# Splitting the product A22 T4 by quarters as well, in blocks two and three

## Chip, core and metric

One core of a Trainium2 chip. The metric is the device time of one launch in microseconds, median of the runs. The engines are called as in the profile: PE (TensorE matmuls), PEld (its weight loads), DVE (VectorE), ACT (ScalarE), POOL (GpSimd), SP (the queue that issues nearly all DMAs).

## What is computed

Local attention over 3072 tokens, then a dense layer pair, then a soft mixture of eight experts whose gate is balanced by eight Sinkhorn rounds. The change lies in the last stage alone:

```python
for e in range(8):
    h = np.maximum(x @ w1[e], 0.0)      # 3072x512 @ 512x1024
    ye = h @ w2[e]                      # 3072x1024 @ 1024x512
    out += P[:, e:e + 1] * ye
```

## The kernel before

The expert stage walks over 24 units `n`: three blocks of 1024 tokens (`sb`), in each eight experts (`e`). Both matrix products of a unit are done by Winograd's form of Strassen's scheme: seven products of half-size matrices instead of eight. Every float32 product is three matmuls in fp32r (`passes`, L225 to L227: high by high, high by low, low by high), each with its own weight load.

For the first product the seven are listed in `FIRST` (weight part, token part, accumulator): 0 is A12 B21 on accumulator b, 1 is A11 B11 on a, 2 is S1 T1 on c, 3 is S2 T2 on a, 4 is S3 T3 on a, 5 is S4 B22 on c, 6 is A22 T4 on a. The accumulators are PSUM tiles that are read out after each product and then added to, so that a product on `a` has to wait until the one before it on `a` has been read.

A plain product takes four steps (`k` = 0 to 3, one per 128 rows of the result), each with six matmuls of 512 columns. Product 0 is split once more: `deep_product` does it as seven sub-products of quarter matrices, again by `FIRST`, in four steps of up to two sub-products (`SUBS`): 1 and 0, 2 and 3, 5 and 4, then 6. A sub-product is six matmuls of 256 columns. The read-outs are in `deep_out` (L876 on ACT, L878 on DVE), those of plain products in `first_out` (L887, L889 on ACT, L891 on DVE); `positive` (L897) takes the Relu, and `gated` (L904) multiplies by the gate on POOL.

A list `order` sets one step of the first product of unit n beside one step of the second product of unit n-1; a unit is 28 steps. In a plain step PE runs six matmuls of the first product and then six of the second. In a deep step it runs a sub-product, half of the second product's step (three matmuls), the other sub-product, and the other half. In the order of the steps of `USES` the deep steps 0, 1 and 2 of product 0 stand first, then two plain steps of product 1, then deep step 3:

```python
    SUBS = ((1, 0), (2, 3), (5, 4), (6,))
    USES = [(DEEP, 0), (DEEP, 1), (DEEP, 2), (0, 1), (DEEP, 3)]
    USES += [(k, p) for k in (0, 2) for p in range(1, 7) if k or p > 1]
```

The weight parts w1 of the next uses are loaded ahead (`w1_load`), rounded to fp32r by ACT (`w1_hi`, L781), and their rest is taken by DVE in block one (`w1_lo`, L786) and stored, and read back in the blocks behind it (`w1_lo_load`). The sums of weight parts (S1 to S4) are made once, on POOL, by the jobs of `factory` during the stages ahead, each a load of 512 KB, four POOL operations (L636) and a store of 512 KB. `gate_load` fetches a unit's gate (tile `pb`). For a new block the token parts are split half by half (`x_half`), those of B21 by quarters (`x_quarters`).

Of the kernel before, what the change touches and what calls it, by code (L numbers as in the profile page):

```python
# [9 lines left out]
F32 = mybir.dt.float32  # L10
# [22 lines left out]
HB = 512  # L33
NEG = -2.0 ** 100
LAG = 2
NG = 14
# [28 lines left out]
def attn_moe_moe(ctx: ExitStack, tc: tile.TileContext, qk, vw, wi, wo, wa, wb, wg, out):  # L65
# [538 lines left out]
    DEEP = "deep"  # L604
    QUART = {"B11": 0, "B21": 1, "B22": 2, "T1": 3, "T3": 4, "T4": 5, "T2": 6}
    SUBS = ((1, 0), (2, 3), (5, 4), (6,))
    USES = [(DEEP, 0), (DEEP, 1), (DEEP, 2), (0, 1), (DEEP, 3)]
    USES += [(k, p) for k in (0, 2) for p in range(1, 7) if k or p > 1]
    NW = 16 * NM
# [14 lines left out]
    def factory():  # L624
# [27 lines left out]
    def quarter_tile():  # L652
        xo["B21"] = xo_p.tile([128, 2, 7, 256], F32R, tag="xoB21", name="xo", bufs=1)

    def quarter_parts(names, raw):
        t, at = xo["B21"], QUART[names[0]]
        hi, lo = (t[:, v, at:at + len(names)].rearrange("p a t -> p (a t)") for v in range(2))
        nc.scalar.activation(out=hi, in_=raw, func=AF.Copy)
        nc.vector.tensor_tensor(out=lo, in0=raw, in1=hi.bitcast(F32), op=ALU.subtract)
# [4 lines left out]
    def x_quarters(r0, r1, eng=nc.vector):  # L664

        l, h = slice(0, 256), slice(256, 512)
        quarter_tile()
        quarter_parts(("B11",), r0[:, l])
        quarter_parts(("B21", "B22"), r1)
# [4 lines left out]
        quarter_parts(("T1", "T3"), r0)  # L674
# [4 lines left out]
        quarter_parts(("T4", "T2"), r1)  # L679
        yield  # L680

    def x_ops(sb, p, tag):
# [24 lines left out]
        yield from x_quarters(xq["B21"][:, 0], xq["B21"][:, 1])  # L707
# [24 lines left out]
    def x_half_load(sb, r):  # L732

        if r < 14:
# [18 lines left out]
    def w1_use(g):  # L753
        return g // 16 % NE, *USES[g % 16]

    def w1_load(g):
        if g < NW:
            e, k, p = w1_use(g)
            s = w1s[g] = w1s_p.tile([128, 2, 256], F32, tag="w1s", name="w1s", bufs=4)
            wk = wa[4 * e:4 * e + 4].rearrange("k p (a f) -> p k a f", a=4)  # L760
            if k == DEEP and p in (1, 2):
                for j in range(2):
                    nc.sync.dma_start(out=s[:, j].rearrange("p (k f) -> p k f", k=2),
                                      in_=quarter(ws3[e], W3S[S1 + 2 * p - 2 + j]))
            elif k == DEEP:
# [590 lines left out]
```

## Time and profile before

| what | value |
|---|---|
| median of 3 runs | 2508.99 us (2508.58 to 2509.62) |
| the profiled execution's own time | 2509.49 us |
| its span, first to last instruction | 2507.7 us |
| busy PE, PEld | 2493.5 us, 2164.3 us |
| busy DVE, ACT, POOL | 1790.2 us, 1416.9 us, 978.1 us |
| mean granted TensorE clock | 1.000 |
| DMA moved | 569.84 MB, mean 227 GB/s |
| expert stage | from about 659 us to the end |

Block one of the expert stage ends near 1246 us, block two near 1856 us. A matmul's end is modelled, so two that follow each other overlap in the rows; what a matmul costs is the distance from its start to the start of the next.

### The profile page before, as it was taken

How to read it: one execution, taken by the hardware profiler on the slowest of the kernel's cores; microseconds unless marked ns; L12 is line 12 of the kernel's file. 1: busy time of each engine (PE TensorE's matmuls, PEld its weight loads, DVE VectorE, ACT ScalarE, POOL GpSimd, SP SyncE). 2: the span in 40 equal slices, each digit the busy share in tenths (PEclk: the TensorE clock that was granted, in tenths of full speed). 3: DMA queues.
4: the chain of work that ended last, by engine and by line, in shares of the span. 5: the costliest groups of instructions: out<-in, count | busy, mean ns of one | idle time of the engine just before them, and what ended most of it. 6: DMA issues, size and time to landing. Idle time of an engine off the chain costs nothing.

```text
span 2507.7 us, 36585 instructions
## 1 busy us (share of the span) xinstructions
PE 2493.5 (99%) x13237; PEld 2164.3 (86%) x13237; DVE 1790.2 (71%) x2252; ACT 1416.9 (57%) x2611; POOL 978.1 (39%) x729
## 2 busy tenths in 40 slices
PE   9999999999999999999999999999999999999999
PEld 8999999999878888888888888888888888888887
DVE  8777656576699999999975656566675566666567
ACT  8666652222365655556666555655566656555554
POOL 0155656454025544433443424333333334233331
PEclk9999999999999999999999999999999999999999
DMA  8689988676466676667777777666686666666654
GB/s 210 188 264 307 288 268 275 228 268 216 135 222 212 237 230 240 227 222 231 248 232 246 236 230 239 226 214 215 218 272 214 221 219 213 202 216 210 213 189 148
DMA packets 344305, 569.84 MB, mean 227 GB/s; under 512 B 28531, under 2 KB 198716, under 8 KB 344124
## 3 DMA queue, kind: packets, MB, share of 16 engines
q1 hardware_dynamic: 343840, 567.28, 69.6%
q8 instruction: 103, 1.69, 0.3%
q14 instruction: 78, 0.64, 0.1%
q10 hardware_dynamic: 284, 0.24, 0.0%
HBM read 434.13 MB, written 133.27 MB: 226 GB/s over the span
## 4 chain that ended last, share of the span: by engine, by line
PE 94%; DVE 4%; ACT 1%; DMA 1%; issue 1%; ACTq 0%; SPq 0%; DVEq 0%
PE ga L225 8%; PE ga L227 7%; PE ga L226 7%; PE oa L226 7%; PE oa L225 7%; PE oa L227 7%; PE gc L225 4%; PE pa L225 4%; PE gc L226 4%; PE gc L227 4%; PE oc L226 4%; PE ph L225 4%; PE pa L227 3%; PE pa L226 3%; PE oc L227 3%; PE oc L225 3%
## 5 line engine op out<-in xcount | busy, mean ns | idle before, releaser
L904 POOL TENSOR_TENSOR g<-g,pb 128x512 f32<-128x512 f32 x368 | 637.1, 1745 | 1148.2 <-ACT g L897 1060.2
L940 ACT ACTIVATE oh<-g 128x1024 fp32r<-128x1024 f32 x336 | 355.0, 1056 | 508.6 <-issue 191.7
L945 DVE TENSOR_TENSOR ol<-g,oh 128x1024 fp32r<-128x1024 f32 x336 | 448.1, 1334 | 207.5 <-ACT oh L940 207.3
L225 PE MATMUL ga<-xo,w1h 128*128 128x512 f32 (+1 forms) x960 | 355.0, 370 | 1.0 <-DVE g L878 0.6
L227 PE MATMUL ga<-xo,w1l 128*128 128x512 f32 (+1 forms) x960 | 353.1, 368 | 0.0
L226 PE MATMUL ga<-xo,w1h 128*128 128x512 f32 (+1 forms) x960 | 353.0, 368 | 0.0
L636 POOL TENSOR_TENSOR fr<-fr 128x256 f32<-128x256 f32 x288 | 252.0, 877 | 176.9 <-DMA fr<-in_wa_dram 90.4
L226 PE MATMUL oa<-ol,w2h 128*128 128x512 f32 x760 | 297.2, 391 | 1.4 <-DVE ol L945 1.4
L225 PE MATMUL oa<-oh,w2h 128*128 128x512 f32 x760 | 296.6, 390 | 0.0
L227 PE MATMUL oa<-oh,w2l 128*128 128x512 f32 x760 | 295.8, 389 | 0.0
L920 DVE TENSOR_TENSOR g<-g 128x1024 f32<-128x1024 f32 x192 | 265.0, 1420 | 0.0
L781 ACT ACTIVATE w1h<-w1s 128x512 fp32r<-128x512 f32 (+1 forms) x384 | 233.6, 608 | 5.6 <-DMA w1s<-ws 5.6
L897 ACT ACTIVATE g<-g 128x512 f32<-128x512 f32 x288 | 178.3, 619 | 80.3 <-DVE g L891 80.0
L225 PEld LDWEIGHTS ga<-xo,w1h 128*128 128x128 f32 x960 | 180.5, 188 | 38.2 <-ACT g L876 1.7
L398 ACT ACTIVATE t<-ph,half 128x384 f32<-128x384 f32 x128 | 74.7, 584 | 244.2 <-PE ph L227 237.9
L226 PEld LDWEIGHTS ga<-xo,w1h 128*128 128x128 f32 x960 | 180.5, 188 | 33.0
L227 PEld LDWEIGHTS ga<-xo,w1l 128*128 128x128 f32 x960 | 180.4, 188 | 30.1
L974 DVE TENSOR_TENSOR y<-y,oa 128x512 f32<-128x512 f32 x172 | 117.3, 682 | 121.2 <-PE oa L227 121.1
L818 ACT ACTIVATE w2h<-w2s 128x1024 fp32r<-128x1024 f32 x168 | 177.2, 1055 | 46.8 <-DMA w2s<-ws 19.2
L891 DVE TENSOR_TENSOR g<-g,ga 128x512 f32<-128x512 f32 x192 | 130.6, 680 | 78.1 <-PE ga L227 78.0
L225 PE MATMUL gc<-xo,w1h 128*128 128x512 f32 (+1 forms) x480 | 177.3, 369 | 1.0 <-ACT g L876 1.0
L227 PE MATMUL gc<-xo,w1l 128*128 128x512 f32 (+1 forms) x480 | 176.5, 368 | 0.0
(174 smaller groups left out, 5448.9 us busy)
## 6 DMA issues: line engine op xcount, KB each, us to landing
w1l<-wl SPq DMA_DIRECT2D x240, 256.0 KB, 4.0
w2l<-wl SPq DMA_DIRECT2D x112, 512.0 KB, 3.7
w1s<-ws SPq DMA_DIRECT2D x192, 256.0 KB, 4.7
w2s<-ws SPq DMA_DIRECT2D x96, 512.0 KB, 5.2
ws<-fr SPq DMA_DIRECT2D x72, 512.0 KB, 5.5
w2s<-in_wb_dram SPq DMA_DIRECT2D x144, 256.0 KB, 4.7
wl<-w1l SPq DMA_DIRECT2D x120, 256.0 KB, 4.5
wl<-w2l SPq DMA_DIRECT2D x56, 512.0 KB, 4.5
```

The costliest lines, as they stand in the source:

```text
L225: nc.tensor.matmul(ps, wh, xh, start=start, stop=False, skip_group_check=more)
L226: nc.tensor.matmul(ps, wh, xl, start=False, stop=False, skip_group_check=more)
L227: nc.tensor.matmul(ps, wl, xh, start=False, stop=stop, skip_group_check=more)
L636: nc.gpsimd.tensor_tensor(out=o, in0=a, in1=b, op=f)
L781: nc.scalar.activation(out=w1_part(g, w1[g]), in_=w1_part(g, w1s[g]), func=AF.Copy)
L818: nc.scalar.activation(out=hi, in_=w2s[m], func=AF.Copy)
L891: nc.vector.tensor_tensor(out=g, in0=g, in1=ps, op=ALU.add)
L897: nc.scalar.activation(out=g, in_=g, func=AF.Relu)
L904: nc.gpsimd.tensor_tensor(out=g, in0=g, in1=p, op=ALU.mult)
L920: nc.vector.tensor_tensor(out=o, in0=gq[n, x, i], in1=gq[n, y, i], op=ALU.subtract)
L940: nc.scalar.activation(out=hi, in_=gq[n, b, i], func=AF.Copy)
L945: nc.vector.tensor_tensor(out=lo, in0=gq[n, b, i], in1=op[m, i].bitcast(F32), op=ALU.subtract)
```

## The change

In units 8 to 23 (blocks two and three) product 6, A22 T4, is no longer four plain steps but the four deep steps `DEEP2`, the last of the unit: with the same sub-products in the same pairs, but in one row, with nothing between step 2 and step 3. Unit 8's T4 is not split by halves ahead but by quarters (`x_quarters` with form "T4"), whose last three parts lie in a tile `more`. What product 4 leaves on `a` is now copied to B21 by ACT as well (`more` in `first_out`), and the seven sub-products are added to it by DVE (`deep_out`); ACT's Relu of B21 moves to `positive`. `factory` gets a ninth kind of job (tile `ws4`), so 80 jobs in place of 72, begun every 1.27 steps instead of 1.4. The ring of `w1h` has four tiles instead of five, and the gate has one tile in place of two, loaded in step (0, 1) of its own unit instead of step (2, 1) of the unit before.

```diff
-    wl1 = [dr_p.tile([128, 2, 256], F32, name=f"wl1{g}") for g in range(16 * NE)]
+    wl1 = [dr_p.tile([128, 2, 256], F32, name=f"wl1{g}") for g in range(20 * NE)]
+    ws4 = [dr_p.tile([128, 4, 256], F32, name=f"ws4{e}") for e in range(NE)]
...
+    DEEP, DEEP2 = "deep", "deep2"
+    FORM = {DEEP: "B21", DEEP2: "T4"}
+    QUART = {"B21": 0, "B22": 1, "T1": 2, "T3": 3, "T4": 4, "T2": 5, "B11": 6}
     SUBS = ((1, 0), (2, 3), (5, 4), (6,))
+    USES0 = [(DEEP, 0), (DEEP, 1), (DEEP, 2), (0, 1), (DEEP, 3)]
+    USES1 = USES0 + [(k, p) for k in (0, 2) for p in range(1, 6) if k or p > 1] + [(DEEP2, r) for r in range(4)]
+    USES0 += [(k, p) for k in (0, 2) for p in range(1, 7) if k or p > 1]
...
-            out.append(job(wa[4 * e:4 * e + 4].rearrange("k p (a f) -> p k a f", a=4)[:, :, A12 + 1], ws3[e], OF_W3,
-                           quarter))
+            for a, ws in ((A12, ws3), (A22, ws4)):
+                out.append(job(wa[4 * e:4 * e + 4].rearrange("k p (a f) -> p k a f", a=4)[:, :, a + 1], ws[e], OF_W3,
+                               quarter))
...
+    def quarter_tile(form):
+        if form == "T4":
+            xo[form] = xo_p.tile([128, 2, 2, HB], F32R, tag="xoT4", name="xo", bufs=1)
+            xo["more"] = pb_p.tile([128, 2, 3, 256], F32R, tag="more", name="more", bufs=1)
...
-        if r < 14:
+        if r < 12:
...
-        return w1r_p.tile([128, 2, 256], F32R, tag=f"w1{t}", name=f"w1{t}", bufs=AHEAD + (t == "h"))
+        return w1r_p.tile([128, 2, 256], F32R, tag=f"w1{t}", name=f"w1{t}", bufs=AHEAD)
...
-            g = gq[n, "B11", i][:, :, 256 * th:256 * th + 256]
-            if p in (1, 2, 3, 6):
+            g = gq[n, "B11" if d == DEEP else "B21", i][:, :, 256 * th:256 * th + 256]
+            if p in (1, 2, 3, 6) and d == DEEP:
                 nc.scalar.activation(out=g, in_=ps, func=AF.Copy)
             else:
                 nc.vector.tensor_tensor(out=g, in0=g, in1=ps, op=ALU.add)
...
+        more = p == 4 and n >= NE
+        for v in [b] * (p in (2, 3, 6)) + ["B21"] * more:
+            if k % 2 == 0:
+                gq[n, v, i] = g_p.tile([128, 2, HB], F32, tag="g", name="g", bufs=NG)
...
+        if more:
+            nc.scalar.activation(out=gq[n, "B21", i][:, k % 2], in_=ps, func=AF.Copy)
...
-        if b != "B21":
+        if b != "B21" or n >= NE:
             nc.scalar.activation(out=g, in_=g, func=AF.Relu)
...
-            t = pb[n] = pb_p.tile([128, 8, 128], F32, tag="pb", name="pb", bufs=2)
+            if n:
+                t = pb_p.tile([128, 8, 128], F32, tag="pb", name="pb", bufs=1)
...
-        starts = [15 + 1.4 * j for j in range(len(jobs))]
+        starts = [15 + 1.27 * j for j in range(len(jobs))]
...
-            for stage_, late in ((2, 3), (0, 0), (1, 1.5)):
+            for stage_, late in ((2, 2.6), (0, 0), (1, 1.3)):
...
+                if h[1] == DEEP2 and p > 1:
+                    after = [(n, 2 * p - 4 + j, "B21") for j in range(2)]
...
-                if (k, p) == (0, 1) and n == 2:
-                    gate_load(2)
-                if (k, p) == (2, 1) and n >= 2:
-                    gate_load(n + 1)
+                if (k, p) == (0, 1) and n >= 2:
+                    gate_load(n)
```

Two places of the order of instructions, both from a unit of block two. First PE at the end of a unit. Before, the second half of the second product's step on `oa` stands between A22 T4 for one `k` and for the next (`ga` is the accumulator, `xo` the tokens, `w1h` and `w1l` the weights):

```order
L225 MATMUL oa_16259<-oh_16789,w2h_16744 128x512
L226 MATMUL oa_16259<-ol_16814,w2h_16744 128x512
L227 MATMUL oa_16259<-oh_16789,w2l_16746 128x512
L225 MATMUL ga_16637<-xo_13624,w1h_16711 128x512
L226 MATMUL ga_16637<-xo_13624,w1h_16711 128x512
L227 MATMUL ga_16637<-xo_13624,w1l_16709 128x512
```

The accumulator there is one that the step before did not touch. After the change (lines are one further down) the same engine has, at the end of sub-product 4, through the half step to sub-product 6:

```order
L226 MATMUL ga_15655<-xo_13770,w1h_15602 128x256
L227 MATMUL ga_15655<-xo_13770,w1h_15602 128x256
L228 MATMUL ga_15655<-xo_13770,w1l_15644 128x256
L226 MATMUL oa_15099<-oh_15640,w2h_15587 128x512
L227 MATMUL oa_15099<-ol_15675,w2h_15587 128x512
L228 MATMUL oa_15099<-oh_15640,w2l_15589 128x512
L226 MATMUL ga_15655<-more_13771,w1h_15652 128x256
L227 MATMUL ga_15655<-more_13771,w1h_15652 128x256
L228 MATMUL ga_15655<-more_13771,w1l_15706 128x256
```

Here sub-product 4 ends and sub-product 6 begins on one and the same tile, `ga_15655`, three matmuls apart. Second, DVE over the same steps. Before, it adds product 5 to the result (L891), adds the second product's results (L974) and takes rests of its operands (L945):

```order
L891 TENSOR_TENSOR g_16727<-g_16727,gc_16665 128x512
L974 TENSOR_TENSOR y_14349<-y_14349,ob_16781 128x512
L891 TENSOR_TENSOR g_16727<-g_16727,gc_16687 128x512
L974 TENSOR_TENSOR y_14854<-y_14854,oa_16259 128x512
L945 TENSOR_TENSOR ol_16881<-g_16241,oh_16860 128x1024
```

After it, the additions of sub-products 2, 3, 5 and 4 (L902) stand there, with the rest of one weight part (L810, in block two only); L1006 is the second product's addition:

```order
L902 TENSOR_TENSOR g_15569<-g_15569,gc_15685 128x2x256
L810 TENSOR_TENSOR w1l_15706<-w1s_15506,w1h_15652 128x256
L902 TENSOR_TENSOR g_15338<-g_15338,ga_15655 128x2x256
L902 TENSOR_TENSOR g_15338<-g_15338,gc_15685 128x2x256
L902 TENSOR_TENSOR g_15569<-g_15569,ga_15655 128x2x256
L1006 TENSOR_TENSOR y_15039<-y_15039,oa_15099 128x512
```

The fifth row is the reading of `ga_15655` that the last product on that tile has to wait for.

## Rows read from the trace of the kernel before

**Rows 1.** Page, part 1: busy time of each engine, share of the span and instructions.

```profile
PE 2493.5 (99%) x13237; PEld 2164.3 (86%) x13237; DVE 1790.2 (71%) x2252; ACT 1416.9 (57%) x2611; POOL 978.1 (39%) x729
```

**Rows 2.** Page, part 4: shares of the span in the chain that ended last, by engine.

```profile
PE 94%; DVE 4%; ACT 1%; DMA 1%; issue 1%; ACTq 0%; SPq 0%; DVEq 0%
```

**Rows 3.** Timeline of PE, one unit of block three: start, duration, then the instruction.

```profile
2080.70 0.28 PE L225 MATMUL ga<-xo,w1h 128*128 128x256 f32 x1
...
2087.74 0.28 PE L225 MATMUL ga<-xo,w1h 128*128 128x256 f32 x1
...
2088.33 0.28 PE L227 MATMUL ga<-xo,w1l 128*128 128x256 f32 x1
2088.45 0.40 PE L225 MATMUL oa<-oh,w2h 128*128 128x512 f32 x1
...
2089.15 0.40 PE L225 MATMUL ga<-xo,w1h 128*128 128x512 f32 x1
...
2091.88 0.39 PE L225 MATMUL ga<-xo,w1h 128*128 128x512 f32 x1
...
2094.60 0.28 PE L225 MATMUL ga<-xo,w1h 128*128 128x256 f32 x1
...
2096.70 0.39 PE L225 MATMUL gc<-xo,w1h 128*128 128x512 f32 x1
...
2156.54 0.28 PE L225 MATMUL ga<-xo,w1h 128*128 128x256 f32 x1
```

**Rows 4.** Busy PE, PEld, DVE, ACT, POOL (count), clock, DMA share, GB/s, by stretch.

```profile
800.00:1200.00 400.00, 400.00 (x1864) 335.09 (x1863) 380.24 (x395) 235.14 (x349) 176.19 (x95) 1.00 0.70 232
1400.00:1850.00 450.00, 450.00 (x2094) 376.90 (x2094) 283.50 (x315) 264.89 (x397) 169.77 (x106) 1.00 0.70 229
2010.00:2390.00 380.00, 380.00 (x1776) 318.56 (x1775) 231.16 (x256) 220.03 (x328) 131.77 (x80) 1.00 0.65 212
```

**Rows 5.** Timeline of DVE around the fifth and fourth sub-product of that unit.

```profile
2087.31 0.69 DVE L878 TENSOR_TENSOR g<-g,gc 128x512 f32<-128x512 f32 x1 [0.19 <-PE gc L227]
2088.65 0.69 DVE L878 TENSOR_TENSOR g<-g,ga 128x512 f32<-128x512 f32 x1 [0.65 <-PE ga L227]
```

**Rows 6.** Timeline of DVE in block one, where PE waits for L878.

```profile
793.88 0.68 DVE L878 TENSOR_TENSOR g<-g,ga 128x512 f32<-128x512 f32 x1
```

**Rows 7.** Timeline of PE at that wait, the start and two weights on.

```profile
794.62 0.39 PE L225 MATMUL ga<-xo,w1h 128*128 128x256 f32 x1 [0.33 <-DVE g L878]
794.84 0.28 PE L226 MATMUL ga<-xo,w1h 128*128 128x256 f32 x1
794.96 0.28 PE L227 MATMUL ga<-xo,w1l 128*128 128x256 f32 x1
```

**Rows 8.** Groups of instructions by line and form: busy, mean ns, idle before.

```profile
L225 PEld LDWEIGHTS ga<-xo,w1h 128*128 128x128 f32 x960 | 180.5, 188 | 38.2 <-ACT g L876 1.7 <-DVE g L878 1.4 <-ACT g L887 1.0
...
L897 ACT ACTIVATE g<-g 128x512 f32<-128x512 f32 x288 | 178.3, 619 | 80.3 <-DVE g L891 80.0
...
L786 DVE TENSOR_TENSOR w1l<-w1s,w1h 128x512 fp32r<-128x512 f32 x120 | 111.4, 929 | 0.0
...
L889 ACT ACTIVATE g<-ga 128x512 f32<-128x512 f32 x96 | 55.9, 583 | 12.2 <-PE ga L227 12.2
```

**Rows 9.** POOL work on factory tiles fr alone, by stretch; clock, DMA share, GB/s.

```profile
150.00:300.00 150.00, 70.70 (x77) 1.00 0.98 301
300.00:450.00 150.00, 85.01 (x101) 1.00 0.82 271
450.00:600.00 150.00, 82.73 (x96) 1.00 0.75 251
```

**Rows 10.** DMA issues: count, KB each, median us from issue to landing.

```profile
w1l<-wl SPq DMA_DIRECT2D x240, 256.0 KB, 4.0
...
ws<-fr SPq DMA_DIRECT2D x72, 512.0 KB, 5.5
...
pb<-pd SPq DMA_DIRECT2D x24, 512.0 KB, 4.5
```

More of the change, by code (lines that the diff above doesn't have):

```diff
@@ L706, in x_ops @@
             yield
-        yield from x_quarters(xq["B21"][:, 0], xq["B21"][:, 1])
+        yield from x_quarters("B21", xq["B21"][:, 0], xq["B21"][:, 1])
     def x_source(sb, n, q):
@@ L775, in w1_part, with w1_low @@
     def w1_part(g, t):
-        return t[:, :1] if w1_use(g)[1:] == (DEEP, 3) else t
+        _, k, p = W1[g]
+        return t[:, :1] if k in FORM and p == 3 else t
+    def w1_low(g):
+        n, k, p = W1[g]
+        at, made = W1_LOW[n % NE, k, p]
+        return wl1[at], made == n
     def w1_hi(g):
@@ L783, in w1_lo @@
     def w1_lo(g):
-        if g < 16 * NE:
+        if g < NW and w1_low(g)[1]:
             lo = w1_p_tile("l")
@@ L857, in deep_product @@
             new, at = p < 3, {A12: 1, A11: 0, A22: 0}.get(a, (a - S1) % 2)
-            xh, xl = (xo["B21"][:, v, QUART[x]] for v in range(2))
+            xh, xl = (quarter_view(FORM[d], v, QUART[x]) for v in range(2))
             for v in {1: "ba", 2: "c"}.get(p, ""):
@@ L1187, in attn_moe_moe @@
         quarters = {1: "B11", 4: "B22", 5: "B12", 6: "B21"}
-        left, after = [], None
+        left, after = [], []
         halves, fours, quarter_work = {}, {}, None
@@ L1196, in attn_moe_moe @@
             base = [h for h, _ in order].index((sb * NE - 1, 2, 1)) - 1
-            for r in range(2, 14):
-                halves[base + 1 + r + 5 * (r > 11)] = [(sb, r)]
+            for r in range(2, 12):
+                halves[base + 1 + r] = [(sb, r)]
             for r in range(2, 4):
                 halves.setdefault(base - 4 + r, []).append((sb, r - 2))
-            fours[[h for h, _ in order].index((sb * NE - 1, DEEP, 3))] = sb
+            fours[[h for h, _ in order].index((sb * NE - 1, DEEP, 3))] = sb, "B21"
+            fours[[h for h, _ in order].index((sb * NE, DEEP, 3))] = sb, "T4"
         ends = {at[NM - 1, 0, 0] + d: s for d, s in
@@ L1247, in attn_moe_moe @@
                     store(*left.pop(0))
-            if after:
-                positive(*after)
-            after = None
-            if h and h[1] == DEEP:
+            for w in after:
+                positive(*w)
+            after = []
+            if h and h[1] in FORM:
                 n, _, p = h
-                deep_out(n, p, 1)
-                g = 16 * n + USES.index((DEEP, p))
+                deep_out(*h, 1)
+                if h[1] == DEEP2 and p > 1:
+                    after = [(n, 2 * p - 4 + j, "B21") for j in range(2)]
+                g = W1_AT[h]
                 if g:
@@ L1275, in attn_moe_moe @@
                     w1_lo_store(g + AHEAD - 2)
-            if h and (h[1] == DEEP or h[1] % 2):
-                if h[1] != DEEP:
+            if h and (h[1] in FORM or h[1] % 2):
+                if h[1] not in FORM:
                     w1_load(g + AHEAD + 3)
@@ L1284, in attn_moe_moe @@
                     t = out_p.tile([128, HB], F32, tag="o", name="xs", bufs=NO)
[L1285 removed]
+                    nc.sync.dma_start(out=t, in_=x_source(*fours[i], q))
                     rows.append(t)
[L1287 removed]
+                quarter_work = i + 3, x_quarters(fours[i][1], *rows, nc.gpsimd)
             elif quarter_work and i >= quarter_work[0] and (i - quarter_work[0]) % 2 == 0:
```

95 lines of the change are left out of this document (50 added, 45 removed).

## The prediction

> **What bounds the kernel now.** I read the busy times first: PE is busy for 2493.5 of 2507.7 us, 99% [rows 1]. In the chain that ended last PE has 94% and the next engine, DVE, 4% [rows 2]. So a change is worth what it does to PE's own stream, or what it makes PE wait for. The stretches confirm that for the last stage: in each of the three blocks PE is busy for the whole of it, at clock 1.00, while DVE has 95% in block one (380.24 of 400), 63% in block two and 61% in block three, ACT 58 to 59%, POOL 35 to 44% [rows 4]. Block one, which the change leaves as it is, shows that a DVE at 95% still does not hold PE up as a rule.
>
> The third view is PE's timeline, where only starts count. A unit of block three begins at 2080.70 and the next at 2156.54, so 75.84 us [rows 3]. Twelve matmuls of 512 columns go from 2091.88 to 2094.60: 2.72 us for a plain step, 227 ns a matmul. Six of 256 columns go from 2087.74 to 2088.45: 118 ns a matmul, 0.71 us a sub-product [rows 3].
>
> **What the change removes from PE.** Four plain steps of A22 T4, 4 x 2.72 = 10.88 us a unit, become four deep steps. The unit has those already: steps 0 to 2 take 2080.70 to 2089.15 = 8.45 us, step 3 takes 2094.60 to 2096.70 = 2.10 us [rows 3], together 10.55. The halves of the second product are in both. That is 0.33 us less a unit and 16 x 0.33 = 5.3 us less in all, since units 8 to 23 have it. Seven eighths of the arithmetic give so little because 42 narrow matmuls at 118 ns cost 4.97 us where 24 wide ones at 227 ns cost 5.44, and the three wide ones behind a narrow one run a little slower, 0.70 us from 2088.45 to 2089.15 [rows 3].
>
> The Trainium skill, in "TensorE: Matmul & The Clock Gate", section "Back-to-back issue gap", gives the isolated spacing as N/2.4 + 2.5 ns, 109 and 216 ns for the two widths. By it a unit would save 24 x 215.8 - 42 x 109.2 = 595 ns, an estimate from that page, and the sum below would end at 2505.1. The rows have 118 and 227, and the rows decide.
>
> **What it adds to PE: one wait a unit.** In the deep steps of B21 two plain steps stand between step 2 and step 3. In those of T4 nothing does: sub-product 4 ends step 2, three matmuls of the second product follow, then comes sub-product 6 on the same accumulator. It must wait until DVE has added what sub-product 4 left. The trace has each link. The last matmul of sub-product 4 starts at 2088.33 [rows 3] and DVE's addition of it at 2088.65, 0.32 later, for 0.69 us, on a DVE that had been idle for 0.65 [rows 5]. Where PE does wait for such an addition, it starts 0.06 us after its end: 793.88 + 0.68 = 794.56 [rows 6], and PE at 794.62 [rows 7]. So sub-product 6 can begin 0.32 + 0.69 + 0.06 = 1.07 us after that last start. PE itself is ready at 2089.15 - 2088.33 = 0.82 [rows 3]. The wait is 0.25 us. The first matmul after a wait also takes longer to its follower, 794.62 to 794.84, 0.22 us, where the next takes 0.12 [rows 7]: 0.10 more. Together 0.35 us a unit, 16 x 0.35 = 5.6 us.
>
> The other waits of this kind stay covered. Between sub-products 3 and 4 on `ga`, as between 2 and 5 on `gc`, stand a sub-product and two half steps, about 2.1 us against a need of 1.07. The next unit's first deep step uses other tiles.
>
> **What it adds beside PE.** DVE gets seven additions of 0.69 us [rows 5], 4.8 us a unit, 6.4% of 75.84: block three goes from 61 to 67%. Block two also makes the rests of the new weight parts, three and a half tiles at 0.929 us [rows 8], 3.3 us: 63 to 74%. Both are below the 95% that block one bears. ACT loses four Relus at 0.583 us, gains four copies of about the same and four Relus at 0.619 [rows 8], and one and a half tiles more to round, which I bound by its nearest rows at 0.6 to 0.9 us; some 4 us a unit, from 58 to about 63%. POOL's work per unit is as before, at 131.77 / 80 = 1.65 us an instruction [rows 4]. I cost all this at nothing; the cover is that idle share. If it were gone, an addition of 0.69 us would come late, the second rival.
>
> **SP's queue.** The gate is now fetched in step (0, 1), behind three deep steps. Its one tile is free when POOL has gated the last two parts of B21. They can start once sub-product 6 is added and ACT has taken the Relu, say 1 to 2 us into the new unit, and take 2 x 1.65: free at about 5 us, and the load issues at 8.45. SP therefore should not stop; if it does, the weight loads behind it are for uses several steps ahead. The gate lands 4.5 us after issue [rows 10], and POOL waits for it once a unit, idle there anyway. The ring of four `w1h` still lets ACT round a use ahead of PE by several steps. The added reloads of weight rests are 256 KB each, landing in 4.0 us [rows 10], in stretches where the DMA share is 0.65 to 0.70 [rows 4]. Nothing for either.
>
> **The stages ahead.** `factory` has eight more jobs, each a load and a store of 512 KB. The tightest stretch is 150 to 300 us: DMA share 0.98 at 301 GB/s, with 77 POOL operations, some 19 jobs [rows 9]. One job in 1.27 steps instead of 1.4 is 10% more, two jobs, 2.1 MB, 7 us of DMA time at that rate, against 0.02 x 150 = 3 us of room. So up to 4 us of transfers come late there. Behind it the share is 0.82 and 0.75 [rows 9], room of 27 and 37 us, which takes the delay up. The price for PE lies between 0, where the loads are issued earlier than needed by more than that, and 4 us. I take 0: PE is busy for all of these stretches even at 0.98, and a store that lands late (5.5 us now [rows 10]) has no reader before the last stage. A small gain isn't excluded at block boundaries either, as T4's last load and split leave the crowded steps there; nothing prices it, and I hold it to under 1 us in each of two.
>
> **The sum.** -5.3 + 5.6 + 0 = +0.3 us on the profiled execution's 2509.49, which is 0.5 above the median of 2508.99. On the median: **2509.3 us**, no change. A measurement of this kernel can tell about 0.2%, 5.0 us, from no change: faster is below 2504.0, slower above 2514.0.
>
> **Rivals.** *The wait is hidden.* If sub-product 6 does not in fact wait (DVE reads an accumulator in two parts and is quicker, or what PE still has in hand covers it), the saving stands alone: 2508.99 - 5.3 = 2503.7, just past the line. For it: the wait by my sum is only a quarter of a microsecond. Against: the accumulator is one tile by the order, and each link is a measured one. The spacing could also be better than the rows of block three say, with the wait in place; that ends near 2505.
>
> *DVE is behind when sub-product 4 ends.* Its idle time before that addition is 0.65 us today [rows 5]; with a further addition of 0.69 us in the step, or one weight rest of up to 0.929 us in block two [rows 8], that can be used up. From the point where DVE reaches the addition later than 0.32 us after PE, each us is one of PE's. One addition late in every unit is 16 x 0.69 = 11 us: 2520. Against it: DVE is at 67 to 74%, and the row before that addition in the order is that of sub-product 5, which ended 1.4 us earlier.
>
> *The stages ahead become late.* If PE waits there for all of the 4 us: 2513.3, and with a boundary or two over the line, near 2515. For it speaks the share of 0.98; against it that PE has no wait at this share now.
>
> *The weight loads do not fit.* The Trainium skill, same page, Part 3, section "The mechanism", says that a weight load overlaps matmuls in flight only where their row groups differ. As a mechanism of this kernel: 18 more loads a unit at 188 ns [rows 8], 16 x 18 x 0.188 = 54 us, 2563. The trace speaks against it: narrow matmuls start 118 ns apart [rows 3], each with its load of 188, so the loads lie beside the stream.
>
> **How the numbers follow.** Forecast, saving and wait cancel within 2 us either way: 0.64. Wait hidden: 0.15, half of it on each side of the line. Better spacing with the wait: 0.04, all within. DVE behind: 0.09, of which a quarter, a partial lateness, stays within the line. Stages ahead late: 0.07, half over the line. Loads not fitting: 0.01. Faster: 0.075 and 0.025 for a boundary gain on top, 0.10. Slower: 0.07 + 0.035 + 0.01, with 0.015 for unforeseen waits, 0.13. The rest, 0.77, is no change. The range from 2503.5 to 2515 takes in the hidden wait below and the late transfers above; it leaves out most of the DVE case and the loads.
>
> **What would show it.** In the changed profile PE should have some 288 more matmuls, at 118 and 227 ns from start to start; a unit should still last 75.8 to 75.9 us; in each of the 16 units the first matmul of sub-product 6 should show an idle time of about 0.25 us put down to DVE's addition (L902 there), and only that one. DVE's addition of sub-product 4 should start 0.32 us after the last matmul's start. In 150 to 300 us the DMA share may reach 1.0 with PE still busy throughout. A unit of 75.5 us would make the forecast wrong towards faster; idle time in front of sub-products 4 or 5, additions that start late, or waits of PE ahead of 650 us, towards slower.

## The result and the profile after

The changed kernel takes 2532.45 us (median of 5 runs, 2530.73 to 2533.46) against 2508.99 before: ratio 1.0093, interval 1.0079 to 1.0108. That is 23.5 us slower, 17 us above the range. The profiled execution took 2533.46 us, its span is 2531.6.

Lines of the changed kernel that come up below: L226 to L228 are PE's passes, L902 DVE's addition of a sub-product, L917 of a plain product, L1006 of the second product, L810 the rest of a weight part, L977 the rest and L952 the sum of the second product's operands; L913, L925, L805, L842 and L972 are ACT's read-out, Relu, and roundings of w1, w2 and operands; L932 is POOL's gating; L757, L763 and L768 load, round and take the rest of half token parts, L679 and L682 make quarter parts.

The page's busy times, as in [rows 1]:

```profile
PE 2499.6 (99%) x13525; PEld 2173.8 (86%) x13525; DVE 1931.0 (76%) x2400; ACT 1466.5 (58%) x2711; POOL 1045.3 (41%) x769
```

PE is busy 6 us longer, with modelled ends and stretches at a low clock counted as busy; for the other 18 of the 24 us that the span grew it stands idle. The windows of blocks two and three as in [rows 4], ahead of them the tightest one of the stages ahead (columns: busy PE, PEld, DVE, ACT, POOL with counts, clock, DMA share, GB/s):

```profile
150.00:300.00 150.00, 150.00 (x1213) 141.66 (x1212) 103.54 (x173) 100.10 (x341) 83.81 (x100) 1.00 1.05 314
1400.00:1850.00 450.00, 441.22 (x2131) 369.36 (x2129) 332.50 (x361) 273.01 (x416) 182.78 (x103) 1.00 0.70 231
2010.00:2390.00 380.00, 379.12 (x1862) 319.94 (x1862) 261.92 (x288) 235.38 (x358) 147.38 (x81) 1.00 0.69 221
```

The stages ahead go as forecast: DMA share 1.05 in the tight stretch, PE busy all the time, the last stage begins no later. DVE's shares are the forecast ones as well: 332.50 / 450 = 74% in block two, 261.92 / 380 = 69% in block three. But PE, which had no gap in [rows 4], now misses 8.8 us of the 450 in that window, which takes in the first waits at the change of block. The view of PE's waits names them (instruction that waits, what it waited for, us in total, times, longest). Block two, 1330 to 1800 us:

```profile
PE gc L226 <- DVE g L902: 5.6, 6, 0.9
PE ga L226 <- DVE g L902: 1.1, 6, 0.2
```

Block three, 1990 to 2440 us:

```profile
PE ga L226 <- DVE g L902: 0.9, 5, 0.2
```

The change from block two to three, 1800 to 1900 us, where before PE waited for nothing:

```profile
PE ga L226 <- DVE g L902: 2.9, 2, 2.8
PE gc L226 <- DVE g L902: 2.3, 1, 2.3
PE oa L228 <- DMA w2l<-wl: 1.9, 1, 1.9
PE ga L226 <- ACT g L913: 1.3, 1, 1.3
```

And the end, 2460 us on:

```profile
PE oc L227 <- DVE ol L977: 2.2, 1, 2.2
```

This view counts a wait from the modelled end of the matmul before, so it is short by some 0.15 us each time and leaves out what runs slowly behind a wait. To have all of it I added up, from PE's timeline, what two starts lie apart beyond 237 ns behind a matmul of 512 columns and beyond 121 ns behind one of 256, wherever the surplus is over 40 ns:

| stretch (us) | before | after | more |
|---|---|---|---|
| up to 1280 | 9.8 | 9.5 | -0.3 |
| block two, 1280 to 1800 | 0.6 | 10.6 | 10.1 |
| change of block, 1800 to 1900 | 0.0 | 13.3 | 13.3 |
| block three, 1900 to 2460 | 0.6 | 3.2 | 2.6 |
| the end | 1.7 | 5.1 | 3.4 |
| sum | 12.7 | 41.7 | 29.1 |

29.1 us of surplus less the 5.3 that were to be saved is 23.8; the spans differ by 2531.6 - 2507.7 = 23.9. So the saving is there, and more than five times as much is lost again. Three places have most of it; the end is taken up with the experiments.

**In every unit, in front of sub-product 6.** PE's timeline in block three: the last matmul of sub-product 4, the last of the half step of the second product behind it, the first of sub-product 6, and the same matmul in the next unit (start, duration, instruction, idle time before and its releaser):

```profile
2097.92 0.28 PE L228 MATMUL ga<-xo,w1l 128*128 128x256 f32 x1
...
2098.51 0.39 PE L228 MATMUL oa<-oh,w2l 128*128 128x512 f32 x1
2099.07 0.35 PE L226 MATMUL ga<-more,w1h 128*128 128x256 f32 x1 [0.18 <-ACT w1h L805]
...
2174.96 0.36 PE L226 MATMUL ga<-more,w1h 128*128 128x256 f32 x1 [0.17 <-DVE g L902]
```

DVE's addition in between:

```profile
2098.24 0.69 DVE L902 TENSOR_TENSOR g<-g,ga 128x512 f32<-128x512 f32 x1 [0.72 <-PE ga L228]
```

The addition starts 0.32 us after the last matmul's start, as in [rows 5]; PE restarts 0.56 us after a 512-column matmul that is otherwise followed after 0.23 to 0.24, and 0.14 us after the addition's end (2098.93), where [rows 6] and [rows 7] had 0.06. (One of the two rows names ACT's rounding of a later weight part, which happens to end at the same moment; with the pairs turned, below, PE goes on at 2174.93 without a wait although that rounding runs from 2174.36 to 2175.00 there, so it is the addition that counts.) A unit lasts 2174.96 - 2099.07 = 75.89 us, where 75.8 to 75.9 was forecast. Block three is as predicted.

**In block two, in front of sub-product 5.** It waits for DVE's addition of sub-product 2, 0.9 us by the waits view. PE's last matmul of sub-product 2 and the start of sub-product 5:

```profile
1463.83 0.28 PE L228 MATMUL gc<-xo,w1l 128*128 128x256 f32 x1
...
1467.13 0.39 PE L226 MATMUL gc<-xo,w1h 128*128 128x256 f32 x1 [0.93 <-DVE g L902]
```

DVE over that stretch:

```profile
1460.03 1.23 DVE L977 TENSOR_TENSOR ol<-g,oh 128x1024 fp32r<-128x1024 f32 x1 [0.94 <-ACT oh L972]
1461.17 1.79 DVE L810 TENSOR_TENSOR w1l<-w1s,w1h 128x512 fp32r<-128x512 f32 x1
1462.88 0.68 DVE L917 TENSOR_TENSOR g<-g,gc 128x512 f32<-128x512 f32 x1
1463.48 0.67 DVE L902 TENSOR_TENSOR g<-g,ga 128x512 f32<-128x512 f32 x1
1464.07 1.21 DVE L977 TENSOR_TENSOR ol<-g,oh 128x1024 fp32r<-128x1024 f32 x1
1465.21 0.67 DVE L902 TENSOR_TENSOR g<-g,gb 128x512 f32<-128x512 f32 x1
1465.81 0.68 DVE L1006 TENSOR_TENSOR y<-y,ob 128x512 f32<-128x512 f32 x1
1466.40 0.67 DVE L902 TENSOR_TENSOR g<-g,gc 128x512 f32<-128x512 f32 x1
```

POOL beside it:

```profile
1460.59 3.52 POOL L932 TENSOR_TENSOR g<-g,pb 128x512 f32<-128x512 f32 x2 [3.84 <-ACT g L925]
1464.30 2.15 POOL L932 TENSOR_TENSOR g<-g,pb 128x512 f32<-128x512 f32 x1 [0.19 <-ACT g L925]
```

The addition (1466.40) could have started at 1463.83 + 0.32 = 1464.15 and comes 2.25 us late. DVE has no gap from 1460.03 on. What fills it: six instructions, the longest the rest of a weight part (L810 at 1461.17) that takes 1.79 us while POOL is gating. From 1330 to 1800 us there are 18 such rests: the 12 that lie beside POOL take 1.8 us, the 6 that do not take 0.69. Just before, DVE had stood 0.94 us for ACT, with that rest already possible but queued behind the instruction that waited.

**At the change of block.** Among SP's waits from 1800 to 1870 us are these, both in front of a load of half token parts:

```profile
SPq L757 <- POOL xs L682: 7.7, 1, 7.7
...
SPq L757 <- DVE xo L679: 5.9, 1, 5.9
```

Together 13.6 us in a row, in which SP issues nothing; before, it stood 6.5 us at one of the two. The reason is in the order: with the plain steps of product 6 gone from the first half of a unit, the second half, and these loads with it, starts two steps earlier, while the quarter split of B21, whose tiles the loads are to reuse, stayed at its step. The weights of the second product queue behind. PE waits 1.9 us for them, ACT 6.80 and DVE then 7.14 for ACT's next half:

```profile
1836.26 1.06 ACT L842 ACTIVATE w2h<-w2s 128x1024 fp32r<-128x1024 f32 x1 [6.80 <-DMA w2s<-in_wb_dram]
```

and on DVE

```profile
1838.87 0.69 DVE L768 TENSOR_TENSOR xo<-xs,xo 128x512 fp32r<-128x512 f32 x1 [7.14 <-ACT xo L763]
```

When all of it goes on, the half splits (L768) and T4's additions are due together, and the rests beside POOL run long again. DVE has no gap from 1851.20 to 1864.74; from it, the long ones and the two additions that PE waits for (2.8 and 2.3 us):

```profile
1853.01 2.09 DVE L977 TENSOR_TENSOR ol<-g,oh 128x1024 fp32r<-128x1024 f32 x1
1855.02 1.77 DVE L810 TENSOR_TENSOR w1l<-w1s,w1h 128x512 fp32r<-128x512 f32 x1
...
1857.91 0.68 DVE L902 TENSOR_TENSOR g<-g,ga 128x512 f32<-128x512 f32 x1
...
1859.11 2.31 DVE L977 TENSOR_TENSOR ol<-g,oh 128x1024 fp32r<-128x1024 f32 x1
...
1862.54 0.67 DVE L902 TENSOR_TENSOR g<-g,gc 128x512 f32<-128x512 f32 x1
```

The clock adds to it. PE has half the clock, 1.2 GHz, in three stretches of this trace: from 1832.1 to 1835.6, behind the wait of 1.9 us; from 1859.5 to 1866.3, behind the wait of 2.8 us and through the one of 2.3 us; and from 2490.9 to 2494.3, behind the wait of 2.2 us. A window out of each:

```profile
1832.00:1835.00 3.00, 3.00 (x9) 2.29 (x8) 0.00 (x0) 0.00 (x0) 0.00 (x0) 0.52 0.83 227
1864.00:1866.00 2.00, 2.00 (x9) 1.71 (x8) 1.79 (x4) 0.00 (x0) 0.00 (x0) 0.50 0.58 202
2491.00:2494.00 3.00, 3.00 (x9) 2.00 (x8) 3.00 (x3) 0.00 (x0) 0.37 (x1) 0.50 0.51 165
```

A 512-column matmul then starts 0.43 us behind another (1833.60, 1834.03, 1834.45) in place of 0.23. In the table above this is in the surplus: some 1.5 us in each of the three places. Not all of that is a loss of its own. With the edit "DVE's order alone" below, which changes nothing at the end, the same wait of 2.2 us has no low clock behind it:

```profile
2486.00:2490.00 4.00, 3.17 (x13) 2.30 (x14) 4.00 (x4) 0.00 (x0) 1.36 (x1) 1.00 0.54 188
```

PE then waits 0.5 us more for DVE, and the surplus of the end is 4.8 us against 5.1. So the length of a wait alone does not tell whether the clock falls, and at the end the low clock costs about 0.3 us. The five executions of the changed kernel differ in it too: a mean clock of 0.997 in the three of 2532.45 to 2533.46 us, 0.999 in the two of 2530.73 and 2531.58. Behind the 0.9 us waits of block two the clock stays at 1.00.

### The profile page after: what moved, and what is told of

It reads as the page before. It is cut to its first block, busy times and chain, and to the rows that moved or that the text cites. A ratio compares the mean times of both kernels' runs of the same rounds, so it can differ in the third digit from the quotient of the medians.

```text
span 2531.6 us, 37953 instructions
## 1 busy us (share of the span) xinstructions
PE 2499.6 (99%) x13525; PEld 2173.8 (86%) x13525; DVE 1931.0 (76%) x2400; ACT 1466.5 (58%) x2711; POOL 1045.3 (41%) x769
## 5 line engine op out<-in xcount | busy, mean ns | idle before, releaser
L932 POOL TENSOR_TENSOR g<-g,pb 128x512 f32<-128x512 f32 x368 | 679.5, 1865 | 1118.0 <-ACT g L925 904.0
L972 ACT ACTIVATE oh<-g 128x1024 fp32r<-128x1024 f32 x336 | 354.9, 1056 | 414.5 <-PE oa L228 196.3
L977 DVE TENSOR_TENSOR ol<-g,oh 128x1024 fp32r<-128x1024 f32 x336 | 461.1, 1373 | 135.7 <-ACT oh L972 135.4
L644 POOL TENSOR_TENSOR fr<-fr 128x256 f32<-128x256 f32 x320 | 268.6, 840 | 191.2 <-DMA fr<-in_wa_dram 103.1
L226 PE MATMUL ga<-xo,w1h 128*128 128x512 f32 (+1 forms) x864 | 314.3, 364 | 2.4 <-ACT g L913 1.3
L228 PE MATMUL ga<-xo,w1l 128*128 128x512 f32 (+1 forms) x864 | 312.7, 362 | 0.0
L227 PE MATMUL ga<-xo,w1h 128*128 128x512 f32 (+1 forms) x864 | 312.6, 362 | 0.0
L228 PE MATMUL oa<-oh,w2l 128*128 128x512 f32 x760 | 296.6, 390 | 1.9 <-DMA w2l<-wl 1.9
L226 PE MATMUL oa<-oh,w2h 128*128 128x512 f32 x760 | 298.0, 392 | 0.0
L952 DVE TENSOR_TENSOR g<-g 128x1024 f32<-128x1024 f32 x192 | 289.6, 1548 | 0.0
L805 ACT ACTIVATE w1h<-w1s 128x512 fp32r<-128x512 f32 (+1 forms) x416 | 250.2, 601 | 40.3 <-issue 21.3
L925 ACT ACTIVATE g<-g 128x512 f32<-128x512 f32 x352 | 215.0, 620 | 84.8 <-DVE g L917 84.6
L226 PE MATMUL gc<-xo,w1h 128*128 128x512 f32 (+1 forms) x544 | 196.8, 362 | 9.5 <-DVE g L902 8.5
L842 ACT ACTIVATE w2h<-w2s 128x1024 fp32r<-128x1024 f32 x168 | 176.9, 1053 | 38.6 <-DMA w2s<-in_wb_dram 25.6
L228 PE MATMUL gc<-xo,w1l 128*128 128x512 f32 (+1 forms) x544 | 194.7, 358 | 0.0
L227 PE MATMUL gc<-xo,w1h 128*128 128x512 f32 (+1 forms) x544 | 194.7, 358 | 0.0
L226 PEld LDWEIGHTS ga<-xo,w1h 128*128 128x128 f32 x864 | 162.8, 188 | 36.2 <-ACT g L900 2.5
L227 PEld LDWEIGHTS ga<-xo,w1h 128*128 128x128 f32 x864 | 162.8, 188 | 28.7
L228 PEld LDWEIGHTS ga<-xo,w1l 128*128 128x128 f32 x864 | 162.6, 188 | 25.2
L1006 DVE TENSOR_TENSOR y<-y,oa 128x512 f32<-128x512 f32 x172 | 117.2, 681 | 87.1 <-PE oa L228 86.9
```

Of the source, the lines that this page charges most:

```text
L226: nc.tensor.matmul(ps, wh, xh, start=start, stop=False, skip_group_check=more)
L227: nc.tensor.matmul(ps, wh, xl, start=False, stop=False, skip_group_check=more)
L228: nc.tensor.matmul(ps, wl, xh, start=False, stop=stop, skip_group_check=more)
L644: nc.gpsimd.tensor_tensor(out=o, in0=a, in1=b, op=f)
L805: nc.scalar.activation(out=w1_part(g, w1[g]), in_=w1_part(g, w1s[g]), func=AF.Copy)
L842: nc.scalar.activation(out=hi, in_=w2s[m], func=AF.Copy)
```

## The experiments

Theory one: the loss is made by T4's deep steps themselves, in the three places above and at the end, by waits that differ in kind, so that each has an edit of its own that removes it and the edits add up. The rivals are named in each expectation. Each median stands beside that of the kernel before from the same chip, with the ratio and its interval. "Less" without more is against the 2532.45 us of the changed kernel, beside which the kernel before had 2508.99; on the other chips it has up to 0.9 us more. The surplus is that of the table above. The first question is whether the product itself or what came with it has cost the time.

**Everything but the product.** The kernel before with four tiles for `w1h`, one gate tile, nine kinds of jobs and their pace:

```diff
+            t = pb_p.tile([128, 8, 128], F32, tag="pb" if n else "pb0", name="pb", bufs=1)
...
+        starts = [15 + 1.27 * j for j in range(len(jobs))]
...
-        return w1r_p.tile([128, 2, 256], F32R, tag=f"w1{t}", name=f"w1{t}", bufs=AHEAD + (t == "h"))
+        return w1r_p.tile([128, 2, 256], F32R, tag=f"w1{t}", name=f"w1{t}", bufs=AHEAD)
```

> The kernel before (A22 T4 in four plain steps) with all that the change brings beside the product: the ring of w1h with four tiles, one gate tile loaded in step (0, 1), the ninth kind of factory job and its denser pace. Theory one (the 23 us come from the split product itself: an addition that sub-product 6 waits for, DVE behind in block two, SP stopped at the change from block two to block three, a later end): no change, 2507 to 2511 us, and PE without waits between 1330 and 1900 us. Rival (weights, gates or factory transfers come late through the shorter rings and the denser pace): 2515 us or more, with waits of PE for w1h or of POOL for pb in every unit.

2508.95 us against 2509.47, ratio 0.9999 (0.999 to 1.0008). Block two again without a gap:

```profile
1400.00:1850.00 450.00, 450.00 (x2095) 376.90 (x2094) 295.19 (x314) 265.57 (x397) 173.77 (x107) 1.00 0.70 229
```

So ring, gate, jobs and their transfers cost nothing, and the loss belongs to the product's steps with what serves them alone and is not in this kernel: T4's quarter split, its weight rests and ACT's copies.

**DVE without T4's rests in block two.**

```diff
+        if k == DEEP2:
+            return wl1[W1_LOW[n % NE, DEEP, p][0]], False
```

> The changed kernel, but in block two DVE does not take the rests of T4's weights; in blocks two and three the rests of A12's quarter parts are loaded in their place (so the low parts of A22's quarters are left out). Theory one: the wait of sub-product 5 in block two (1.08 us and 0.10 for the restart, six units) goes, a unit there lasts 75.9 in place of 77.1 us, and the stop at the change of block stays for the most part: 2521 to 2526 us. Rival (all of DVE's lateness, also the 13 us around 1830 to 1868, comes from these rests): 2508 to 2514 us.

2523.86 us against 2509.47, 8.6 less, ratio 1.0058 (1.0046 to 1.0071). Of block two's waits only one kind is left:

```profile
PE ga L226 <- DVE g L904: 1.1, 6, 0.2
```

The wait of sub-product 5 is gone from all six units (the surplus there falls from 10.6 to 3.5 us); the change of block keeps 10.3 of 13.3. That is theory one.

**POOL without gating in block two.**

```diff
+        if not NE <= n < 2 * NE:
+            nc.gpsimd.tensor_tensor(out=g, in0=g, in1=p, op=ALU.mult)
```

> The changed kernel without POOL's gate multiplications in block two (units 8 to 15 go ungated; the gate tiles are still loaded). Theory one (DVE is late in front of T4's deep steps because its instructions run long beside POOL: the rests of weight parts 1.42 us on average there, 0.69 where POOL is idle): in block two the rests take 0.7 us, L952 1.2, the wait of 1.18 us in front of sub-product 5 goes, and the change of block from two to three loses a part: 2517 to 2525 us. Rival (the sheer number of DVE's instructions makes it late): no more than 2 us less, 2530 to 2533.

2516.98 us against 2509.85, ratio 1.0029 (1.0017 to 1.004), 15.5 less than the changed kernel, just below what was expected. The same groups of DVE from 1330 to 1800 us, first in the changed kernel (count, busy us, mean ns):

```profile
L952 DVE TENSOR_TENSOR g<-g 128x1024 f32<-128x1024 f32 x50 | 80.2, 1644 | 0.0
...
L810 DVE TENSOR_TENSOR w1l<-w1s,w1h 128x512 fp32r<-128x512 f32 x18 | 25.5, 1417 | 0.0
L902 DVE TENSOR_TENSOR g<-g,ga 128x512 f32<-128x512 f32 x30 | 20.4, 680 | 7.6 <-PE ga L228 7.6
```

and without gating (L953 is L952 there):

```profile
L953 DVE TENSOR_TENSOR g<-g 128x1024 f32<-128x1024 f32 x50 | 62.9, 1300 | 0.0
...
L902 DVE TENSOR_TENSOR g<-g,ga 128x512 f32<-128x512 f32 x30 | 20.6, 688 | 11.5 <-PE ga L228 11.5
...
L810 DVE TENSOR_TENSOR w1l<-w1s,w1h 128x512 fp32r<-128x512 f32 x18 | 12.4, 687 | 0.0
```

The rests go from 1417 to 687 ns, the sums from 1644 to 1300, and with as many instructions as before DVE is on time: sub-product 5 does not wait, the surplus in block two falls to 3.5 us and at the change of block from 13.3 to 3.9. The additions from PSUM (L902) take 0.68 and 0.69 us. At the change of block more goes than DVE's long instructions: SP's wait of 7.7 us for POOL's quarter split and PE's wait for the second product's weights are gone too, so this run does not say how much of the 9.4 us there is which. The Trainium skill, "SBUF — State Buffer", section "SBUF: two separate sides", says that VectorE and GpSimd have one pair of ports in common, taken by one of them for a whole instruction, and that VectorE needs it for an instruction with two inputs in SBUF. The rows agree: L810 and L952 have two such inputs and run long beside POOL, L902 has one input in PSUM and does not.

**DVE's order alone.** In block two's plain steps the rests stand ahead of the operands:

```diff
+            while lows and h and NE <= h[0] < 2 * NE:
+                do, n = lows.pop(0)
+                do(n)
             for m in makes.get(i, ()):
                 make(*m)
```

> The changed kernel with one thing moved: in the plain steps of block two DVE takes the rests of weight parts ahead of the rests of the second product's operands, not behind them. Theory one (DVE is not full there, it stands in the wrong order: before the rest L977 at 1460.03 it waits 0.94 us for ACT, and the rest of a weight part that takes 1.79 us comes only then): the wait in front of sub-product 5 shrinks from 1.18 to some 0.2 us a unit, 2525 to 2528 us. Rival (DVE is full at the end of a unit, whatever the order): 2531 to 2533.

2527.95 us against 2509.60, ratio 1.0073 (1.006 to 1.0086), 4.5 less. In block two no wait of sub-product 5 remains (six waits of 0.2 us in front of 6), the surplus falls from 10.6 to 3.5 us, as much as with the rests taken away. At the change of block it rises from 13.3 to 16.0. So DVE was not full in block two, it stood in the wrong order; a better order and the absence of POOL's multiplications each cure that wait by themselves.

**Pairs turned.** No two sub-products on one accumulator closer than a sub-product and two halves:

```diff
-    SUBS = ((1, 0), (2, 3), (5, 4), (6,))
+    SUBS = {DEEP: ((1, 0), (2, 3), (5, 4), (6,)), DEEP2: ((1, 0), (3, 2), (4, 5), (6,))}
```

> The changed kernel with the deep steps of T4 as 1 and 0, 3 and 2, 4 and 5, then 6, so that a sub-product and two halves stand between any two on one accumulator. Theory one: the 0.33 + 0.07 us in front of sub-product 6 go in all units (a unit of block three 75.5 in place of 75.9), in block two the 1.08 us pass from sub-product 5 to sub-product 4: 2525 to 2527.5 us. Rival (PE waits for something else there, such as weights, or the wait is passed on whole): 2531 to 2533.

2527.10 us against 2509.47, ratio 1.0072 (1.0059 to 1.0085), 5.4 less. Two units of block three, by the first matmul of T4's sub-product 1:

```profile
2166.49 0.28 PE L226 MATMUL ga<-more,w1h 128*128 128x256 f32 x1
...
2241.98 0.28 PE L226 MATMUL ga<-more,w1h 128*128 128x256 f32 x1
```

75.49 us, against 75.84 before: this is the saving without the wait, 0.35 us a unit where 0.33 was forecast. In block two the wait passes to sub-product 4 as expected (4.9 us in six). (The profiled execution took 2531.39 us, the longest of the five, so its trace serves for these waits and units and not for the time.)

**Half loads two steps later.**

```diff
-                halves.setdefault(base - 4 + r, []).append((sb, r - 2))
+                halves.setdefault(base - 4 + r + 2 * (sb == 2), []).append((sb, r - 2))
```

> The changed kernel with the first two loads of half token parts for block three issued two steps later, where they stood to the quarter parts before the change. Theory one: SP no longer stands 13.6 us at these two loads with the weights of the second product behind them; the waits of PE at 1830 and 1840 and the low clock behind them go, DVE's waits at 1858 and 1863 shrink: 2518 to 2525 us. Rival (DVE is simply overloaded there): at most 2 us less, 2530 to 2533.

2530.43 us against 2509.47, ratio 1.0083 (1.0069 to 1.0096): 2.0 less, where runs of one kernel spread by 2 to 3. The expected 7 or more did not come. (The profiled execution reaches the same load of w1s at 1799.66 in place of 1797.68, so 2 us of its time went before this place; its granted clock was at half from 17.5 to 20.9 us.) The waits from 1800 to 1900 us show both sides:

```profile
PE ga L226 <- DVE g L902: 2.9, 2, 2.8
PE gc L226 <- DVE g L902: 2.7, 1, 2.7
PE oa L227 <- DVE ol L977: 0.8, 1, 0.8
```

The waits for w2l and for ACT, 1.9 and 1.3 us, are gone, so SP's stop made those, and the surplus falls from 13.3 to 9.2. The two of DVE stay: there the half splits, T4's rests and seven additions are due in the same steps, whether SP stands or not. The time is the rival's; by the waits each theory is right for a part.

**The three cures together.** The three edits shown above: pairs turned, half loads later, and T4's rests taken away from DVE in block two:

> Three edits together on the changed kernel: the pairs of T4 turned, the half loads for block three two steps later, and in block two no rests of T4's weights taken by DVE (A12's are loaded in their place, the low parts of A22's quarters are left out). Theory one (the parts lie in different places and add up): 2532.5 - 5.4 - 2.0 - 8.6 = 2516.5, within 1.5 us; what is left is DVE's lateness around 1855 and the later end. Rival (they are one shortage of DVE that a few edits already cure): under 2512.

2513.92 us against 2509.60, ratio 1.0016 (1.0007 to 1.0025): 18.5 less, 2.6 below the sum of the three and outside what either theory had written, nearer to theory one. What is left is one wait at the change of block (4.7 us, the surplus 6.7) and the end (4.6).

**A complete version.** Pairs turned, half loads later, rests first, and the last four half splits behind T4's steps:

```diff
-                halves[base + 1 + r] = [(sb, r)]
+                halves[base + 1 + r + 5 * (sb == 2 and r > 7)] = [(sb, r)]
```

> The whole change with nothing left out, in four new places: pairs of T4 turned, half loads for block three two steps later, rests of weight parts first in block two's plain steps, and the last four half splits for block three (T3, B22) five steps later, behind T4's deep steps. Theory one: units of blocks two and three 75.5 us, at most 3 us of waits at the change of block, the end still 3.4 us later: 2507 to 2512 us. Rival (the load on DVE at the change of block is only moved to the deep steps of the next unit): 2515 or more.

2516.74 us against 2509.60, ratio 1.0029 (1.0018 to 1.0041). Five units of block two last 75.49 us like those of block three, without a wait. The change of block did not yield: sub-product 3 of unit 15 alone waits 5.8 us, since the additions of product 5 and of sub-product 1 stand behind long rests on DVE. Theory one missed; the time is the rival's, but the load did not move to the deep steps of the next unit: the long wait is still in unit 15.

**The end.** As the last, with the Relu and gating of B21 in the last unit eleven steps later:

```diff
+                    if n == NM - 1:
+                        held[i + 11], after = after, []
```

> As repaired, and in the last unit the Relu and gating of B21 moved eleven steps back, so that POOL's four gatings do not run beside DVE's sums and rests of the last operands (3.97 and 3.91 us there now for two, 2.35 each without POOL). Theory one: PE's wait at 2490 falls from 2.3 us below 1 and the low clock behind it goes: 2 to 4 us less than repaired, 2504 to 2509. Rival (the end is later since B21 itself comes later): as repaired, within 1 us.

2514.88 us against 2509.60, ratio 1.002 (1.0011 to 1.0029), 1.9 less than without this edit: just under the 2 to 4 expected and no more than the spread of such runs, and above 2504 to 2509. The trace shows what it does. DVE's sums and rests at the end, in the changed kernel:

```profile
2484.05 3.97 DVE L952 TENSOR_TENSOR g<-g 128x1024 f32<-128x1024 f32 x2
...
2488.54 3.91 DVE L977 TENSOR_TENSOR ol<-g,oh 128x1024 fp32r<-128x1024 f32 x2
```

the gatings themselves

```profile
2482.87 8.50 POOL L932 TENSOR_TENSOR g<-g,pb 128x512 f32<-128x512 f32 x4 [6.87 <-ACT g L925]
```

and DVE with the edit:

```profile
2466.04 2.48 DVE L952 TENSOR_TENSOR g<-g 128x1024 f32<-128x1024 f32 x2
...
2469.03 2.35 DVE L977 TENSOR_TENSOR ol<-g,oh 128x1024 fp32r<-128x1024 f32 x2
```

From 3.97 and 3.91 us to 2.48 and 2.35. PE's wait of 2.2 us there falls to 0.5, no low clock follows, the surplus of the end falls from 4.5 in the version without this edit to 1.9, where the kernel before has 1.7. The later end was POOL beside DVE, not B21's lateness.

**ACT's copy first.** The program lets the two readings of what product 4 leaves follow each other, ACT's copy behind DVE's addition; the edit turns them:

```diff
+        if more:
+            nc.scalar.activation(out=gq[n, "B21", i][:, k % 2], in_=ps, func=AF.Copy)
         if p in (2, 3):
...
-        if more:
-            nc.scalar.activation(out=gq[n, "B21", i][:, k % 2], in_=ps, func=AF.Copy)
```

> The changed kernel with one thing moved: of the two readings of what product 4 leaves, ACT's copy to B21 stands ahead of DVE's addition to B22, so that ACT waits for PE and not for DVE there. Theory one (the two readings of one accumulator are taken one after the other; ACT stood up to 3.2 us behind DVE there around 1840, and DVE then 1.7 us for ACT's next half part): only the change of block gains, 2 to 5 us less, 2527 to 2531 us. Rival (ACT's late copy costs nothing, DVE is full): 2531.5 to 2533.5.

2526.53 us against 2509.13, ratio 1.0069 (1.0055 to 1.0083), 5.9 less, a little more than expected, and not only at the change of block (surplus 13.3 to 10.0): in block two the wait of sub-product 5 falls from 0.9 to 0.4 us. I had not expected that part; the two traces show where it comes from, though no run tests it. In the changed kernel ACT's copy at 1457.93 has waited 3.09 us for DVE's addition, the rounding of operands comes behind it, DVE waits the 0.94 us for that rounding, and the rest of the weight part then falls beside POOL (1.79 us). With the copy first DVE does not wait there, and the same rest, at 1459.04, falls into a gap of POOL's gating and takes 0.68 us.

**The same in the complete version,** the edit of the end and this one together:

> repaired_tail and ACT's copy first. Theory one: the 5.9 us in front of sub-product 3 at the change from block two to three fall to 1 to 3 and the low clock behind them goes: 2509 to 2512.5 us. Rival (the load on DVE, not the order, makes them): 2514 to 2516.

2514.80 us against 2509.13, ratio 1.0022 (1.0013 to 1.0031): nothing gained on top of the complete version. The time is the rival's. The trace is mixed: the wait of sub-product 3 falls from 5.8 to 4.1 us, so the order has a part in it, but the low clock lasts twice as long in this execution, and in block two sub-product 4 now waits 0.2 to 0.3 us in each unit (the surplus there rises from 2.3 to 4.9).

**And six half splits seven steps later,** in place of four five steps later:

```diff
-                halves[base + 1 + r + 5 * (sb == 2 and r > 7)] = [(sb, r)]
+                halves[base + 1 + r + 7 * (sb == 2 and r > 5)] = [(sb, r)]
```

> As repaired_copy, with six half splits (T2 too) seven steps later in place of four five steps later. Theory one: less of DVE's work is left beside the deep steps of T4, 1 to 2 us less than repaired_copy: 2507 to 2511. Rival (it comes back in the deep steps of the next unit, where ACT reads out sub-products): 1 to 4 us more than repaired_copy.

2513.79 us against 2509.13, ratio 1.0019 (1.001 to 1.0028): 1.0 less than the last, at the edge of what was expected and within the spread. The wait at the change of block is 3.3 us. This is the fastest complete version, 4.7 us above the kernel before; no version beat the kernel before.

## Why the prediction was wrong

- **The saving: right.** 0.33 us a unit forecast, 75.84 - 75.49 = 0.35 measured where no wait follows.
- **The wait in front of sub-product 6: right.** 0.25 + 0.10 forecast, 0.33 + 0.07 measured, with the link of 0.32 us from matmul to addition confirmed and the one from addition to PE 0.14 in place of 0.06. Block three alone would have given "no change".
- **The stages ahead, the gate, the ring: right.** Taken at 0, measured 0.9999 with all of them and without the product. (The DMA share rose to 1.05, so the 3 us of room, reckoned up to a share of 1.0, were no bound.)
- **"The other waits of this kind stay covered": this step failed**, with "I cost all this at nothing; the cover is that idle share". The share itself was forecast to a per cent or two (74 and 67%, measured 74 and 69%). But I compared the need, 1.07 us, with 2.1 us of PE's work as if DVE were free when the sub-product ends. In block two it is 2.25 us behind at that point; its idle time lies elsewhere in the unit. That is worth 7 of the 24 us (six waits of about 1.2 us): with the order of DVE alone changed, the surplus of block two falls by 7.1.
- **A mean duration hid it.** "Three and a half tiles at 0.929 us" [rows 8] is the mean over block one of instructions that take 0.69 us alone (about 90 of the 120) and 1.8 beside POOL (26). In block two, where 12 of 18 lie beside the gating, the mean is 1.42. POOL's work was not "as before" either: its 81 instructions in block three take 147.38 us, where 80 took 131.77.
- **The change of block was not walked through.** I wrote that T4's last load and split leave the crowded steps there and held a gain of under 1 us in each of two. In fact 13.3 us are lost at one. The order of steps shows the shift before any run: with the plain steps of product 6 gone, the second half of a unit comes two steps earlier against work that is tied to the first. I counted the two loads that disappear and not the steps that move. "SP therefore should not stop" was worked out for the gate alone; there it stood 13.6 us for the half loads, and weights of the second product came 1.9 us late.
- **The end** (3.4 us) and **the low clock** behind some of the longer waits were not in the sum at all.
- **The rival that came true** was "DVE is behind", with the right mechanism, at the wrong sub-product, at 11 us and a chance of 0.09. Its price was one addition late in every unit; what is late is a queue of six instructions, and at the change of block PE waits for DVE 2.8 and 2.3 us, more than twice the 0.9 of a unit of block two.

What stays open: how the last 3 to 6 us at the change of block divide between DVE's load and its order, why ACT's copy first, which alone gains in block two, costs it 2.7 us together with the rests first, and what besides the length of a wait decides whether the clock falls. Whether a placement exists that turns the 0.35 us a unit into a gain was not found; all of it would be 5 us.

## What to carry to other kernels

An engine's idle share over a unit is no cover for a wait at one place in it: walk its queue through the stretch in question, with durations of that stretch, and see how late it already is when the new work arrives. When steps disappear from an order, list what moves earlier with what follows them and what stays tied to a step; the loads that wait for each other's tiles are where it shows. A mean over a mixed group (here 0.69 alone, 1.8 beside POOL) is two durations, and which of them holds depends on the neighbour.

## What was not expected of the hardware

DVE's instructions with two inputs in SBUF take 687 ns without POOL's multiplications and 1417 ns on average with them, the same instructions in the same places; those with an input in PSUM keep 680 to 688 ns. And a wait of PE can cost more than itself: in the changed kernel the granted clock fell to half behind waits of 1.9, 2.8 and 2.2 us, so that a 512-column matmul took 0.43 us from start to start, while behind the waits of 0.9 us nothing of the kind is seen. It does not follow every such wait: with DVE's order changed, the same 2.2 us at the end were followed by a clock of 1.00.
